# Another order of all instructions for a dilated convolution with a gate, on one core

## Chip, cores and metric

The kernel runs on one core of a Trainium2 chip. The time is the device time of one execution in microseconds (us). Five engines work on their own instruction queues, each in order: TensorE (PE in the profile; its weight loads are PEld), VectorE (DVE), ScalarE (ACT), GpSimd (POOL) and SyncE (SP), which here only issues transfers.

## What is computed

```
B, T, D, K = 2, 16000, 256, 3            # x: (B, T, D), w: (K, D, 2D), w_o: (D, D), bf16
h[t] = x[t] @ w[0] + x[t-2] @ w[1] + x[t-4] @ w[2]      # x is zero before its start
f, g = h[..., :D], h[..., D:]
z = tanh(f) * sigmoid(g)
return z @ w_o
```

A causal convolution over time with three taps and dilation 2, for each of the two batches, a gate, and one more product.

## The kernel before

**Groups.** The 32,000 rows are cut into 23 groups (`GROUPS`, `ORDER`). 18 are of kind A (6 x 256 rows), 4 of kind B (4 x 256 rows, the last one 4 x 160) and one, the first, of kind P, done by plain products. A group's input `xt` comes transposed from DRAM by a transfer that SP issues (token `x`), so that channels lie on the partitions.

**Fewer products by sums.** Kinds A and B don't multiply every tap with every row. They form sums and differences of input tiles first and multiply these with combined weights (as in fast convolution by Toom-Cook points), then take the outputs apart again. For a group of kind A the tiles are `u0, u1, u2, e, f` (differences and sums of two views of `xt`), three scaled copies of `u1` (`u3` = u1/3, `uh` = -u1/2, `ud` = 2 u1), and four tiles made on top of others: `rp` = f + u1, `rm` = e + u3, `r0` = u0 + uh, `ri` = u2 + ud. Each tile is 128 x 1024. The scaled copies are DVE's (L329). A sum is one DVE instruction of 128x1024 or four GpSimd pieces of 128x256 (L331), the pieces held until a named DVE instruction is done. The four "on top" tiles are mostly made by a transfer that GpSimd issues and that adds its source onto the tile in SBUF (L326, `u<-uh` and the like in the profile).

**Products.** Every group has four blocks (one per 128 columns of `h`). A block of kind A is five products of two matmuls 128x512 on PE (L360): F (`wa` x u1), M (`wm` x rm), L (`wp` x rp), Z (`w[2]` x r0) into a PSUM bank `b`, and I (`w[0]` x ri) into a bank `a`. Between them the banks are read: ACT copies `b` to `ss` (token `c`, L391); the sum `a` = 3 ss + b (token `A`, L394, DVE), the second product `hh` and the sum `yy` (token `Y`, L394, DVE). `hh` has two forms: `h`, a DVE sum 1.5 ss - b, or `k`, a plain copy of `b` by ACT (L404):

```python
if on_act:
    G["k", oi] = True
    nc.scalar.copy(out=G["hh", oi][:, :n], in_=G["b", oi][:, :n])
    return
stt(G["hh", oi][:, :n], G["ss", oi][:, :n], 1.5, G["b", oi][:, :n], ALU.subtract)
...
if ("k", oi) in G:
    stt(G["y", oi][:, :n], G["hh", oi][:, :n], -2.0, G["a", oi][:, :n])
else:
    stt(G["y", oi][:, :n], G["hh", oi][:, :n], 2.0, b)
```

With `k` the sum `yy` reads bank `a` (and I, which adds to that bank, stands behind it); with `h` it reads bank `b` (and Z stands behind it). ACT then takes tanh or sigmoid of `b`, `yy` and `a` (L442; `th`, `sg`), DVE multiplies the two to `zz` (the gate, token `g`, L461), PE multiplies `zz` with `w_o` (token `P`, four matmuls 128x256, L479), ACT or DVE takes the result out of PSUM (tokens `e` on ACT, L496; `v` on DVE, L488) and SP stores it. PSUM has two banks for `a`, three for `b`, three for `o_ps`.

**What sets the order.** A list written out by an offline planner, `PLAN`, of some 1,730 tokens. The kernel goes through it once and emits each token's instructions; every engine runs its own in that order, and semaphores, derived from who reads and writes which tile, hold an instruction until its inputs and its buffer are free. A token with `q` and a number is one GpSimd piece, with how far back the DVE instruction lies that it is held behind; a token that ends in `d` is an adding transfer. So the list sets the order on each engine and the splits (DVE or GpSimd, `h` or `k`, `e` or `v`), not times.

Of the kernel before, what the change touches and what calls it, by code (L numbers as in the profile page):

```python
# [23 lines left out]
d3.2q11 L A d3.2q12 Z I g b Z p.2 a I b m.2 F d3.2q1 P A c F ri.0d rp.0 a I e2 e.0 L e3 Z uh.0 c wa.14q1 P A b rm.0d  # L24
P d0.2 e4 Z a g I s2 e5 F s0 u1.1 x b L u2.1 d3.2q1 P c A F a L u0.0 wa.10q34 c Z A I b wa.8q3 L u1.2 a Z uh.1 F b
ud.1 wa.3q1 I A c F r0.0d g a x L c u0.1 Z e6 P u2.2 b M u3.1 I ud.2 k0 F g wa.5q1 a L A c P wa.13q47 e7 A Z
wa.15q25 e8 M wa.11q2 Y b I wa.9q4 s3 k1 f.1 Z ri.1d a F e.1 L c g I rm.1d b M A rp.1d F k2 f.2 r0.1d P c Y P y M
e.2 a L h3 e9 u1.3q1 Z A y I u1.3q3 L b Y P u1.3q27 a Y F e10 u1.3q55 I A c ri.2d Z e11 u3.2 M e.3 b rm.2d Z uh.2 y
rp.2d F g b P c u0.2 F k4 M f.3 r0.2d a I h5 c L u0.3q41 y P A rp.3d M a u0.3q46 L Y e12 P k6 Y Z y A I b L u3.3 e13
I ud.3 rm.3d g a F Z c u1.4q17 A P y M u1.4q51 Y b P u1.4q77 v14 k7 Z a F e.4 s7 b L x g I c f.4q70 F y A M c  # L30
u0.3q49 v15 P k8 M f.4q9 Y a L h9 f.4q61 e16 Z x e17 A f.4q44 P b L u1.4q53 Y I e18 uh.3 F a u2.4q73 Y Z c P u0.3q32
A b I u2.3 r0.3d y Z u3.4 F y g rm.4d M b I c h10 F e19 u0.4 M a L h11 e.5q85 c P y A ri.3d P e20 L Y e.5q55 M a s9
Y I x k12 u2.4q96 A Z a P f.5 b L u1.5 e21 Z e22 F A I b u3.5 P c Y u2.5q56 F y g rp.4d M c Z u2.4q21 y h13 P b M
uh.4 u2.5q32 a L h14 F e23 u2.5q18 Y I c s10 e.5q60 L A s8 a M u1.6q97 Y e24 P e.5q67 y h15 Z e25 I u2.4q35 A P b
rp.5d e.6 L y r0.4d F g a Z c I uh.5 f.6q1 b A P a M ud.4 u2.5q107 e26 F Y P k16 ri.4d u0.5 s11 Z c g L r0.5d b P
f.6q61 e27 A I y M v29 e28 P u2.6q119 Y a F u2.6q111 h17 P c rm.5d Z ud.5 y L u0.6 ri.5d b M A f.6q110 e30 P Y e31 F
I h18 c u1.6q41 I e32 g M u2.6q35 a Z s13 a h19 x L b P u1.6q62 A L y f.6q34 Y F y I u1.6q22 A c Z u2.6q28 e33 Y P y
rp.6d e.7 P s12 b M g a Z F y h20 u0.7q138 I b u3.6 L c u2.7q95 F A e34 u2.7q119 P e35 Y M rm.6d c P s14 ud.6 a u1.7
Z ri.6d k21 M uh.6 I b g r0.6d P e36 u2.7q79 L h22 a P e37 A F u2.7q30 y L Y u0.7q38 c P A e38 Z u0.7q22 y Y I s15 M
b x ud.7 P u3.7 a e.8q13 h23 Z e39 F g b L c I A e.8q1 e41 F y Y M f.7q56 I c u1.8 rm.7d Z k24 x uh.7 M v40 b  # L40
u0.8q38 L a h25 P f.7q64 y P A u0.7q84 e42 F Y P a L c f.8 f.7q1 Z e44 A I b e.8q8 Y M a F f.7q33 v43 k26 Z g c
rp.7d I b L ri.7d ud.8 M a uh.8 r0.7d F y A P k27 u1.9 P u0.8q1 c Y L y M A u0.8q141 e45 Z y P Y e.8q10 I b e.9
rp.8d Z k28 f.9 F a I u3.8 b L g rm.8d c F e46 u0.8q94 A M c P h29 a u0.9q113 M Y e47 L u0.9q24 y P h30 s18 u2.9q173
Z e48 s17 A I s16 r0.8d b Y x L e49 F g a Z u1.10q148 c P Y b M u3.9 u0.9q156 e50 A I y F u0.9q35 h31 Z a uh.9 L c
e.10 I y f.10q121 A P a M u2.9q126 Y b P u1.10q64 h32 y Z s19 g y r0.9d P F e51 rp.9d ud.9 L b u2.8 P f.10q1 c F A x
e52 I Y c f.10q61 M e53 ri.8 Z u1.10q41 a M h33 b I u2.9q193 h34 y L rm.9 F a P Y c u1.11q130 L e55 A u1.10q159 P y
M A u2.9q40 e56 s20 Z Y I ri.9d b g Z k35 I ud.10 b F v54 L a u0.10 F s21 u1.11q1 c P x A c P uh.10 a f.11q177 M Y
e57 M f.10q205 h36 y Z k37 I u3.10 g L b u1.11q1 L e58 A F a P f.11q30 Y y I u1.11q125 A c Z a rm.10d P Y e59 M
r0.10d e.11 b P s22 rp.10d u2.10 Z k38 I e60 g F b L u0.11 c u1.12q203 P e61 A M e62 F u2.11 u1.12q10 y P h39 c P
f.11q159 Y P e63 M e64 uh.11 ri.10 Z a r0.11d L h40 b u1.12q70 P e65 A I y F Y s24 f.11q59 a L x v66 u1.12q202 Z c A  # L50
I b M uh.12 a F u3.11 k41 Y I rm.11d c g L rp.11d y Z u2.12q144 y A P s23 P a Y M b ud.11 Z k42 f.12 ri.11d F e67 g
L c u1.13q10 I b A M e68 P ud.12 u2.12q170 k43 Y F s25 a P x e.13q141 v69 L c u1.13q192 v70 Z y M A u1.13q56 b I h44
u1.13q143 y F y Y u2.12q33 P c L f.13 Z a u3.12 M e.12 b P k45 g I rm.12d e71 P u2.12q47 Y a L s26 y F A u2.13q9 P
e72 A Z c ri.12d uh.13 I b ud.13 M Y e73 e.13q1 F a h46 Z rp.12d c I u0.12 b L g r0.12d M a F u2.13q107 A k47 P c L
u3.13 u0.13q227 y Y I e74 M e.13q243 A e75 Z s27 e.14q133 h48 P b Y P e.13q204 y F f.14 rm.13d a Z g c L rp.13d I b
u0.13q19 Y P e77 F A a M u2.14q139 v76 c Z e78 u0.13q220 h49 M s28 b I x u1.14 e.14q65 y L h50 F a e.14q155 A P y L
c u0.13q34 Y I e79 A u2.13q15 M y Z Y e.14q244 a P g rp.14d b Z I k51 r0.13d uh.14 F e80 u3.14 L e.15 b P c A
f.15q119 F e81 ud.14 P u2.13q157 y Y M c u0.14 P ri.13d e82 Z u1.15 rm.14d k52 M g I a L b u2.15q51 h53 P a F A
f.15q193 e83 L c u2.15q120 Y s30 P y s29 P A f.15q228 x y M Y u2.14q124 Z e84 h54 I u2.14q230 y Z g b f.15q1 L b F Y
a I u2.14q32 c F A e85 P ri.14d u3.15 y M u1.16 r0.14d Z c h55 P b uh.15 M u0.15q1 a v87 I e86 F g u0.15q123 k56 L  # L60
s31 c P x Y P y u0.15q60 A M e88 u2.15q270 L a h57 Z f.16q173 y A I b u2.15q92 L Y e89 P f.16q46 a Y F s32 u0.15q60
# [586 lines left out]
```

## Time and profile before

| | |
|---|---|
| median of 3 runs | 259.36 us (259.35 to 259.39) |
| profiled execution | 259.23 us, of which the span from first to last instruction is 257.4 us |
| granted TensorE clock | 0.998 |
| busy in the span | PE 250.3, DVE 242.4, ACT 242.4, POOL 179.5 us |
| adding transfers (256 KB each, issued by GpSimd) | 67 |
| transposing loads / stores (issued by SP) | 22 / 46 |

How to read it: a matmul's record lasts longer than the time until the next one starts, since matmuls overlap, so a busy PE can still have lost time; a stall shows as starts that lie further apart than usual. A wait is put down to what ended last. DVE's and ACT's records overlap a little too. Transfers have a time from issue to landing.

### The profile page before, as it was taken

Reading aid. Unit: us, or ns where it says so; the run is one execution under the profiler, and the core shown is the slowest. Engines: PE = TensorE matmul, PEld = TensorE weight load, DVE = VectorE, ACT = ScalarE, POOL = GpSimd, SP = SyncE. Lnnn points to the kernel's source line nnn. Section 1 sums busy time; section 2 is a strip of 40 time slices with the busy share of each in tenths; the row PEclk is TensorE's granted clock in tenths of the full one; section 3 lists DMA queues with packets and bytes.
Section 4 is the critical chain, followed back from the end, with each engine's and each line's share of the span. In section 5 each row is a group of like instructions: output and inputs, shape, how many; then the busy total and the mean of one; then the engine's idle time right before and its main releaser. Section 6 shows DMA issues by size and latency. Waiting matters only on the chain.

```text
span 257.4 us, 4566 instructions
## 1 busy us (share of the span) xinstructions
PE 250.3 (97%) x1428; PEld 137.8 (54%) x1428; DVE 242.4 (94%) x405; ACT 242.4 (94%) x488; POOL 179.5 (70%) x256
## 2 busy tenths in 40 slices
PE   8999999999999999999999999999999999999992
PEld 4644545555555555554554555554555554555681
DVE  2898999999999999999999999999999999999991
ACT  5968999999999999999999999999999999999993
POOL 1133658869689988797886968699899899970000
PEclk9999999999999999999999999999999999999999
DMA  6999899989999999999999989998999986673425
GB/s 186 207 201 219 180 209 242 173 147 194 190 272 273 183 200 278 195 209 214 243 196 288 245 168 201 299 245 179 190 244 243 223 180 135 192 120 131 168 108 190
DMA packets 84752, 52.51 MB, mean 204 GB/s; under 512 B 69080, under 2 KB 70360, under 8 KB 84728
## 3 DMA queue, kind: packets, MB, share of 16 engines
q1 hardware_dynamic: 74168, 33.71, 54.3%
q0 software_dynamic: 9648, 17.57, 40.1%
q10 hardware_dynamic: 912, 0.95, 1.2%
q8 instruction: 11, 0.18, 0.3%
q14 instruction: 13, 0.11, 0.1%
HBM read 1.25 MB, written 16.38 MB: 68 GB/s over the span
## 4 chain that ended last, share of the span: by engine, by line
PE 68%; DVE 9%; POOL 6%; ACT 6%; DMA 5%; issue 3%; ACTq 0%; DVEq 0%; POOLq 0%
PE b L360 40%; PE o_ps L479 14%; PE a L360 10%; DMA e<-u 3%; DMA u<-uh 3%; POOL f L331 2%; ACT sg L442 2%; DVE a L394 2%; DVE yy L394 2%; POOL u L331 2%; PE b L380 1%; PE a L380 1%; ACT osb L496 1%; ACT th L442 1%; ACT ss L391 1%
## 5 line engine op out<-in xcount | busy, mean ns | idle before, releaser
L331 POOL TENSOR_TENSOR u<-xt 128x256 bf16<-128x256 bf16 x92 | 70.1, 775 | 7.8 <-PE a L360 2.4
L479 PE MATMUL o_ps<-wo_sb,zz 128*128 128x256 bf16 x496 | 70.9, 273 | 0.0
L496 ACT CAST osb<-o_ps 128x512 bf16<-128x512 f32 x102 | 62.1, 626 | 0.8 <-PE o_ps L479 0.7
L479 PEld LDWEIGHTS <-zz 128*128 128x128 bf16 x496 | 48.3, 98 | 26.6 <-DVE zz L461 0.4
L394 DVE SCALAR_TENSOR_TENSOR a<-ss,b 128x512 f32<-128x512 f32 (+1 forms) x88 | 59.2, 678 | 2.7 <-PE b L360 1.9
L391 ACT COPY ss<-b 128x512 f32<-128x512 f32 (+1 forms) x88 | 53.3, 608 | 1.1 <-PE b L360 0.6
L360 PEld LDWEIGHTS <-w_sb 128*128 128x128 bf16 x352 | 34.0, 97 | 37.1 <-issue 2.2
L360 PE MATMUL b<-u,w_sb 128*128 128x512 bf16 x144 | 42.8, 379 | 0.4 <-DMA u<-uh 0.2
L360 PE MATMUL b<-f,wp_sb 128*128 128x512 bf16 x144 | 42.6, 379 | 0.3 <-DVE hh L394 0.3
L360 PE MATMUL b<-e,wm_sb 128*128 128x512 bf16 x144 | 42.6, 379 | 0.3 <-DMA e<-u 0.2
L360 PE MATMUL b<-u,wa_sb 128*128 128x512 bf16 x144 | 42.8, 379 | 0.0
L360 PE MATMUL a<-u,w_sb 128*128 128x512 bf16 x144 | 42.2, 379 | 0.0
L461 DVE TENSOR_TENSOR zz<-th,sg 128x1536 bf16<-128x1536 bf16 (+2 forms) x46 | 40.6, 884 | 0.0
L442 ACT ACTIVATE th<-b 128x512 bf16<-128x512 f32 (+1 forms) x44 | 26.9, 612 | 3.8 <-PE b L360 2.2
L394 DVE SCALAR_TENSOR_TENSOR hh<-ss,b 128x512 f32<-128x512 f32 x43 | 29.2, 680 | 1.0 <-PE b L360 0.9
L394 DVE SCALAR_TENSOR_TENSOR yy<-hh,b 128x512 f32<-128x512 f32 x43 | 29.1, 678 | 0.0
L442 ACT ACTIVATE sg<-b 128x512 bf16<-128x512 f32 (+1 forms) x44 | 27.2, 619 | 0.8 <-PE b L360 0.5
L442 ACT ACTIVATE sg<-a 128x512 bf16<-128x512 f32 (+1 forms) x44 | 27.8, 632 | 0.2 <-PE a L360 0.2
L442 ACT ACTIVATE th<-a 128x512 bf16<-128x512 f32 (+1 forms) x44 | 27.0, 615 | 0.4 <-PE a L360 0.3
L331 POOL TENSOR_TENSOR f<-xt 128x256 bf16<-128x256 bf16 x32 | 24.8, 782 | 3.0 <-PE b L360 2.0
L360 PEld LDWEIGHTS <-wp_sb 128*128 128x128 bf16 x176 | 17.2, 98 | 17.9 <-issue 2.9
L360 PEld LDWEIGHTS <-wm_sb 128*128 128x128 bf16 x176 | 17.0, 97 | 14.8 <-issue 1.0
(68 smaller groups left out, 363.0 us busy)
## 6 DMA issues: line engine op xcount, KB each, us to landing
out_dram<-osb SPq DMA_DIRECT2D x36, 384.0 KB, 3.5
e<-u POOLq DMA_DIRECT2D x17, 256.0 KB, 4.1
u<-uh POOLq DMA_DIRECT2D x17, 256.0 KB, 5.4
f<-u POOLq DMA_DIRECT2D x17, 256.0 KB, 5.0
u<-ud POOLq DMA_DIRECT2D x16, 256.0 KB, 4.2
out_dram<-osb SPq DMA_DIRECT2D x8, 256.0 KB, 3.9
w_sb<-in_w_dram ACTq DMA_DIRECT2D x3, 256.0 KB, 4.1
xt<-in_x_dram SPq DMA_TRANSPOSE x22, 8.2
```

The source lines that it names most:

```text
L331: ins = eng.tensor_tensor(out=o, in0=a, in1=b, op=op)
L360: nc.tensor.matmul(G[bank, oi][:, :2 * R], lhsT=wmat[:, ct, osl], rhs=G[mv][:, :, ct, :R], start=which == "first" and ct == 0, stop=ct == ...
L380: nc.tensor.matmul(G[bank, oi][:, :4 * r].rearrange("p (j r) -> p j r", j=4), lhsT=w_taps[tap][:, ct, osl], rhs=xt[:, j0:j0 + 4, ct, c0 + ...
L391: nc.scalar.copy(out=G["ss", oi][:, :n], in_=G["b", oi][:, :n])
L394: return note(nc.vector.scalar_tensor_tensor(out=out, in0=in0, scalar=scalar, in1=in1, op0=ALU.mult, op1=op))
L442: nc.scalar.activation(out=G[name, dt][:, j:j + 2, :R], in_=G[bank, oi][:, :2 * R].rearrange("p (q r) -> p q r", q=2), func=(ACT.Tanh, ACT ...
L461: note(nc.vector.tensor_tensor(out=G["z"][:, dt, :, :n], in0=G["th", dt][:, :, :n], in1=G["sg", dt][:, :, :n], op=ALU.mult))
L479: nc.tensor.matmul(o_ps[:, q, :], lhsT=z, rhs=wo_sb[:, dt, :], start=dt == 0 and (q == 0 or len(dts) == NT), stop=dt == NT - 1, skip_group ...
L496: copy(out=G["osb", at][:, 2 * jp:2 * jp + 2, :], in_=o_ps[:])
```

## The change

Only `PLAN` is replaced; all code, groups and buffers are as before (the new text has one line less, so line numbers in it are lower by one). Its first lines:

```diff
 PLAN = """
-p.0 m.0 d0.0 d3.0 F F c G D w D L c wa.1q1 F A wa.2q4 L c wa.7q5 Z A wa.4q4 I b d3.1 L a F d0.1 I m.1 c Z a A D
-wa.0q1 L x d p.1 wa.12q1 Z b A I b F G Z g c P b u1.0 F a I f.0 e0 L ud.0 a F u2.0 x P c u3.0 P wa.6q1 c A L e1
...
+m.0 d3.0 p.0 F F d0.0 c D c G D L w L A D wa.2q4 F A wa.0q3 d Z c G I b d3.1 L a Z m.1 F d0.1 b wa.4q1 I c A P
+wa.6q11 a F p.1 L c x g I wa.7q1 L A a Z u1.0 P b f.0 I wa.1q1 e0 Z A a P wa.3q11 F b u3.0 rp.0d Z ud.0 c g F L x
...
```

PE has the same matmuls in another order. Counted over the two lists, the splits change so:

| | before | now |
|---|---|---|
| second products as DVE sums (`h`) / ACT copies (`k`) | 43 / 29 | 38 / 34 |
| results taken out by ACT (`e`) / DVE (`v`) | 104 / 22 | 101 / 25 |
| full sums 128x1024 on DVE | 70 | 71 |
| sums for the 160-row group on DVE (128x640) / in GpSimd pieces (128x160) | 0 / 16 | 1 / 12 |
| GpSimd pieces 128x256 | 148 | 148 |
| adding transfers | 67 | 66 |

**At the start, DVE.** The sums for the first group of kind B (`p`, `m`, `d`), the gate of the first group P (`zo`, `zz`, from `th_182,sg_184` and `th_206,sg_208`) and the first sums `a`. Before:

```order
L457 TENSOR_TENSOR zo<-th_182,sg_184 128x128
L461 TENSOR_TENSOR zz<-th_182,sg_184 128x4x128
L394 SCALAR_TENSOR_TENSOR a<-ss,b 128x512 x2
L331 TENSOR_TENSOR d_287<-xt 128x1024
L331 TENSOR_TENSOR d_295<-xt 128x1024
L331 TENSOR_TENSOR m<-xt 128x1024
L394 SCALAR_TENSOR_TENSOR a<-ss,b 128x512
L331 TENSOR_TENSOR p<-xt 128x1024
L394 SCALAR_TENSOR_TENSOR a<-ss,b 128x512
L457 TENSOR_TENSOR zo<-th_206,sg_208 128x128
L461 TENSOR_TENSOR zz<-th_206,sg_208 128x4x128
```

Now:

```order
L456 TENSOR_TENSOR zo<-th_182,sg_184 128x128
L460 TENSOR_TENSOR zz<-th_182,sg_184 128x4x128
L393 SCALAR_TENSOR_TENSOR a<-ss,b 128x512 x2
L456 TENSOR_TENSOR zo<-th_206,sg_208 128x128
L460 TENSOR_TENSOR zz<-th_206,sg_208 128x4x128
L330 TENSOR_TENSOR d_290<-xt 128x1024
L330 TENSOR_TENSOR m<-xt 128x1024
L330 TENSOR_TENSOR d_302<-xt 128x1024
L393 SCALAR_TENSOR_TENSOR a<-ss,b 128x512
L330 TENSOR_TENSOR p<-xt 128x1024
```

The second gate of group P moved from behind four sums of input tiles and two sums `a` to the place right behind the first two sums `a`.

**At the start, ACT.** The first copies and activations of the first group of kind B (`th_285,sg_305` before, `th_288,sg_304` now). Before:

```order
L391 COPY ss<-b 128x512
L442 ACTIVATE sg_305<-a 128x512
L436 ACTIVATE sg_208<-a 128x4x80
L442 ACTIVATE sg_305<-b 128x512
L442 ACTIVATE th_327<-b 128x512
L391 COPY ss<-b 128x512
L442 ACTIVATE sg_345<-b 128x512
L442 ACTIVATE th_327<-a 128x512
```

Now:

```order
L435 ACTIVATE sg_208<-a 128x4x80
L390 COPY ss<-b 128x512
L441 ACTIVATE th_288<-b 128x512
L441 ACTIVATE th_288<-a 128x512
L441 ACTIVATE sg_304<-b 128x512
L390 COPY ss<-b 128x512
L441 ACTIVATE sg_304<-a 128x512
L390 COPY ss<-b 128x512
L441 ACTIVATE th_340<-a 128x512
L441 ACTIVATE th_340<-b 128x512
```

Before, the first activation into the next `th` tile (`th_327`) follows the last of the tile ahead (`sg_305`) directly; now a copy `ss` stands between them, and the last activation of group P (`sg_208`) stands ahead of the first block's activations instead of among them.

**In the middle, GpSimd.** The stretch of pieces and adding transfers for groups of kind A some 80 us into the run. Before:

```order
L326 DMA u_963<-ud 128x1024
L331 TENSOR_TENSOR e<-xt 128x256
L331 TENSOR_TENSOR u_943<-xt 128x256
L331 TENSOR_TENSOR u_1080<-xt 128x256
L326 DMA f<-u_832 128x1024
L331 TENSOR_TENSOR u_943<-xt 128x256
L331 TENSOR_TENSOR u_1080<-xt 128x256 x2
L331 TENSOR_TENSOR e<-xt 128x256
L331 TENSOR_TENSOR u_1137<-xt 128x256
L331 TENSOR_TENSOR e<-xt 128x256
L331 TENSOR_TENSOR u_943<-xt 128x256
L326 DMA f<-u_1053 128x1024
```

Now:

```order
L325 DMA e<-u_972 128x1024
L325 DMA u_978<-uh 128x1024
L325 DMA u_1027<-ud 128x1024
L330 TENSOR_TENSOR u_988<-xt 128x256
L330 TENSOR_TENSOR f<-xt 128x256
L330 TENSOR_TENSOR u_1146<-xt 128x256
L330 TENSOR_TENSOR e<-xt 128x256 x2
L325 DMA f<-u_821 128x1024
```

The transfer `f<-u_821`, whose tile PE reads from its 457th matmul on, is GpSimd's 77th instruction now (pieces, transfers and the fills at the start counted); ahead of it stand three transfers together and five pieces, where before transfers and pieces alternated. Before, the transfer that PE needs nearest to that place (`f<-u_832`, from its 455th matmul on) is GpSimd's 66th.

**At the end, GpSimd.** The last adding transfers and the pieces for the last group (`p`, `m`, `d` of 128x160). Before:

```order
L331 TENSOR_TENSOR u_3188<-xt 128x256 x2
L331 TENSOR_TENSOR e<-xt 128x256
L331 TENSOR_TENSOR f<-xt 128x256
L331 TENSOR_TENSOR p<-xt 128x160
L331 TENSOR_TENSOR e<-xt 128x256 x3
L326 DMA f<-u_2995 128x1024
L326 DMA e<-u_3267 128x1024
L326 DMA u_3271<-ud 128x1024
L331 TENSOR_TENSOR u_3188<-xt 128x256
L331 TENSOR_TENSOR m<-xt 128x160
```

Now:

```order
L330 TENSOR_TENSOR u_3090<-xt 128x256
L330 TENSOR_TENSOR f<-xt 128x256
L330 TENSOR_TENSOR e<-xt 128x256 x2
L330 TENSOR_TENSOR f<-xt 128x256
L325 DMA e<-u_3008 128x1024
L325 DMA f<-u_2990 128x1024
L325 DMA u_3130<-uh 128x1024
L330 TENSOR_TENSOR p<-xt 128x160
L330 TENSOR_TENSOR d_3293<-xt 128x160
L330 TENSOR_TENSOR u_3090<-xt 128x256
L330 TENSOR_TENSOR d_3308<-xt 128x160 x3
```

The transfer onto `e` for the last group of kind A is now GpSimd's 234th instruction, not its 252nd: the pieces of the last group follow it, where before most preceded it, and it is PE's 1,275th matmul that reads the tile first (the 1,283rd before).

More of the change, by code (lines that the diff above doesn't have):

```diff
@@ L27 @@
[L27 to L61, printed above, removed]
```

62 lines of the change are left out of this document (48 added, 14 removed).

## Prediction

> **What bounds the kernel now.** I read the page's busy line first, then the busy times by stage.
>
> ```profile
> PE 250.3 (97%) x1428; PEld 137.8 (54%) x1428; DVE 242.4 (94%) x405; ACT 242.4 (94%) x488; POOL 179.5 (70%) x256
> 0.00:20.00 20.00, 19.06 (x119) 10.70 (x120) 14.14 (x25) 14.32 (x30) 3.91 (x14) 1.00 0.91 195
> 20.00:60.00 40.00, 39.62 (x214) 20.49 (x212) 39.10 (x68) 38.43 (x78) 27.55 (x39) 1.00 1.02 196
> 60.00:120.00 60.00, 59.71 (x337) 32.70 (x336) 59.23 (x100) 59.91 (x121) 50.64 (x71) 1.00 1.11 218
> 120.00:180.00 60.00, 59.95 (x335) 32.45 (x334) 59.86 (x102) 58.86 (x119) 49.75 (x67) 1.00 1.07 232
> 180.00:235.00 55.00, 54.39 (x305) 29.32 (x305) 53.95 (x87) 53.68 (x108) 47.62 (x68) 1.00 0.86 180
> ```
>
> Columns by stage are PE, PEld, DVE, ACT and POOL. From 20 us on three engines are busy 96 to 100% of the time, at the full granted clock; POOL has room until 180 us and little after (47.62 of 55). The matmul's own pace says how much of PE's time is lost:
>
> ```profile
> 8.62 2.50 PE a L380 x18
> 99.19 0.59 PE L360 MATMUL b<-u,wa_sb 128*128 128x512 bf16 x2
> 99.62 0.59 PE L360 MATMUL b<-f,wp_sb 128*128 128x512 bf16 x2
> 100.05 0.60 PE L479 MATMUL o_ps<-wo_sb,zz 128*128 128x256 bf16 x4
> 100.49 0.59 PE L360 MATMUL b<-u,w_sb 128*128 128x512 bf16 x2
> 4.88 2.62 PE b L380 x18
> 251.14 1.47 PE L479 MATMUL o_ps<-wo_sb,zz 128*128 128x256 bf16 x12
> ```
>
> The pairs start 0.43 us apart, so a 512-wide matmul takes 0.215 us; four 256-wide ones take 0.44, so 0.11 each; a 320-wide one 2.50/18 = 0.139. The program has 816 of the first (72 blocks of kind A with 10, 12 full ones of kind B with 8), 500 of the second and 80 of the third: 175.4 + 55.0 + 11.1 = 241.5 us. From 4.88, where the products start, to the last start at some 252.4 are 247.5 us. So PE loses about 6.0 us to waiting (0.3 of it are eight small transposes), spread thinly, and that is all that an order can win; PE's work itself stays. The largest single losses, as the timeline shows them:
>
> ```profile
> 18.81 0.60 ACT L442 ACTIVATE th<-b 128x512 bf16<-128x512 f32 x1 [0.97 <-DVE zz L461]
> 22.38 1.08 PE L360 MATMUL b<-p,wp_sb 128*128 128x512 bf16 x4 [0.39 <-ACT ss L391]
> 200.85 0.61 PE L360 MATMUL b<-u,w_sb 128*128 128x512 bf16 x2 [0.23 <-DMA u<-uh]
> 217.31 0.60 PE L479 MATMUL o_ps<-wo_sb,zz 128*128 128x256 bf16 x4
> 218.02 0.60 PE L360 MATMUL b<-e,wm_sb 128*128 128x512 bf16 x2
> 230.19 0.60 PE L479 MATMUL o_ps<-wo_sb,zz 128*128 128x256 bf16 x4
> 230.97 0.59 PE L360 MATMUL b<-e,wm_sb 128*128 128x512 bf16 x2 [0.17 <-DMA e<-u]
> ```
>
> A bracket is idle time after the last matmul's modelled end, which lies 0.16 us (0.59 - 0.43) behind the pace, so the loss is the bracket plus 0.16: 0.55 at 22.38 and 0.39 at 200.85. At 218.02 and 230.97 the starts lie 0.71 and 0.78 behind four matmuls that take 0.44: 0.27 and 0.34. The other 4.4 us are many waits of a tenth of a microsecond, in which PE, DVE and ACT hold each other.
>
> **Part 1, the start.** PE's wait at 22.38 goes back to ACT, which had stood 0.97 us at 18.81 until the gate of the first group was done on DVE; behind it ACT ran without a pause to the copy `ss` that PE waits for. The list puts that gate ahead of four sums of DVE's, so ACT finds its tile free. Gain at most 0.55, all of PE's wait. Loss at most 0.47: the gate's two instructions now stand ahead of the sums `d` that PE's next products read, and they take
>
> ```profile
> L461 DVE TENSOR_TENSOR zz<-th,sg 128x512 bf16<-128x512 bf16 x4 | 1.7, 418 | 0.0
> L457 DVE TENSOR_TENSOR zo<-th,sg 128x128 bf16<-128x128 bf16 x4 | 0.9, 220 | 0.1
> ```
>
> 0.42 + 0.22 by record, 0.47 by starts (0.34 + 0.13). I take -0.45, near the gain, since PE has products of the same block to run meanwhile.
>
> **Part 2, the transfers at the end.** The chain of waits runs through GpSimd there, from 183 us on:
>
> ```profile
> 187.44 0.71 POOL u L331
> 193.69 0.58 POOL u L326
> 194.27 6.53 DMA u<-uh
> 210.25 1.16 POOL p L331
> 214.66 3.31 DMA e<-u
> 226.82 4.01 DMA e<-u
> ```
>
> GpSimd's pieces take the time, then the transfer that they held back, and then PE is late. How far GpSimd had come at a given matmul is read from counts:
>
> ```profile
> 0.00:79.50 79.50, 78.17 (x439) 41.73 (x440) 72.64 (x124) 72.21 (x146) 47.19 (x75) 1.00 1.02 206
> 79.50:82.50 3.00, 3.00 (x19) 1.73 (x18) 3.00 (x7) 3.00 (x7) 2.68 (x5) 1.00 1.05 192
> 82.50:174.10 91.60, 91.26 (x514) 49.90 (x513) 90.80 (x154) 90.41 (x182) 76.41 (x103) 1.00 1.10 228
> 174.10:226.80 52.70, 52.26 (x292) 28.14 (x291) 51.69 (x82) 51.67 (x105) 49.64 (x70) 1.00 0.89 191
> 226.80:229.30 2.50, 2.50 (x17) 1.47 (x15) 2.50 (x6) 2.50 (x6) 1.56 (x4) 1.00 0.82 138
> ```
>
> (An instruction over a border counts on both sides.) By 226.8 us GpSimd had begun some 250 instructions, and the transfer onto `e`, its 252nd, was the last that PE could wait for. Now that transfer is the 234th, read at the 1,275th matmul, which ran at 229.3: 16 instructions of some 0.7 us (49.64/70), or 11 us, of room. Counted so, transfer by transfer, all from 190 us on have at least five instructions of room now, where before half had three or fewer. The three losses sum to 0.39 + 0.27 + 0.34 = 1.0 and should go. Late next are DVE and ACT: of 55 us they had 1.05 and 1.32 idle, hardly more than the gain. Gain 0 to 1.0; I take -0.7. GpSimd's own four pieces and one transfer less (2 + 0.9 us by its pieces here) lie off the path.
>
> **Part 3, the transfers in the middle.** The opposite holds about 60 and 80 us. The transfer `f<-u_821` is the 77th, and PE reads its tile at the 457th matmul, 82.5 us into the run. At 3.31 from issue to landing, the shortest in the chain above, it must be issued by 79.2, but by 79.5 GpSimd had begun only 75. Two instructions more are 1.4 us, the bound of the loss; the other end is 0, if GpSimd waits less than the 2.18 us that it lost just ahead:
>
> ```profile
> 71.90 0.68 POOL L331 TENSOR_TENSOR u<-xt 128x256 bf16<-128x256 bf16 x1 [2.18 <-PE a L360]
> ```
>
> Some of that wait will stay, since pieces are still held until PE and DVE are done with tiles. I take +0.3, nearer to 0. About 61, 91 and 93 us the same count leaves none to spare.
>
> **Part 4, second products and results.** Pace by starts on a full engine:
>
> ```profile
> 41.88 0.59 ACT L404 COPY hh<-b 128x512 f32<-128x512 f32 x1 [0.18 <-PE b L360]
> 42.38 0.59 ACT L391 COPY ss<-b 128x512 f32<-128x512 f32 x1
> 102.33 0.68 DVE L394 SCALAR_TENSOR_TENSOR hh<-ss,b 128x512 f32<-128x512 f32 x1
> 102.93 0.95 DVE L461 TENSOR_TENSOR zz<-th,sg 128x1536 bf16<-128x1536 bf16 x1
> ```
>
> A second product is 0.50 on ACT and 0.60 on DVE; a result taken out I price the same. ACT: 5 more copies, 3 fewer results, +1.0. DVE: 5 fewer sums, 3 more results, -1.2, one sum 128x1024 and one 128x640 more, some +1.0 at most, so about -0.2. GpSimd's and PE's parts are done above. On the path lies between 0 and the whole 1.0 of ACT, which had 0.09 idle from 60 to 120 us and 1.14 from 120 to 180; below 0 it can't go, since DVE gains almost nothing. I take +0.2, since a full engine slips only where PE stands behind it.
>
> The Trainium skill, "Perfetto Trace Analysis", section "Identifying the Most-Contended Engine", speaks against the change: it says to improve the engine with the highest occupancy first, and for VectorE and ScalarE the occupancy is to be trusted. The trace has both at 94%, and the list loads one of them further; by that rule the whole of ACT's +1.0 would count and nothing of the rest would be won, 260.4. Rival (a) below is this kernel's own form of it.
>
> **Sum.** -0.45 - 0.7 + 0.3 + 0.2 = -0.65. The profiled run took 259.23 us (0.13 under the median of 259.36): 258.6 there, 258.7 as a median.
>
> **Rivals.** (a) ScalarE becomes the bound. Counted in the new order, the 969th matmul, which ran at 174.1, needs ACT's 337th instruction done; by the counts above ACT had begun 333 then (146 + 7 + 182, less two counted twice), the last two under way. So ACT must be some six instructions, 3 us, further at the same place. It had 1.57 + 0.09 + 1.14 = 2.8 us idle from 20 to 180 us and 5.7 ahead of 20. If it can't, PE waits for what is missing: with half of it, +1.5 and without the +0.2, 259.36 - 0.85 + 1.5 = 260.0, slower. It decides if ACT still idles over 0.5 us between 60 and 180. Against it: ACT starts its stretch earlier by part 1. Chance 0.18. (b) Transfers in the middle are late: the four places at 61, 82, 91 and 93 us cost the bound of 1.4 once and 0.4 at each other, +2.6 instead of +0.3: 261.0. It decides if two of the four cost more than 0.5. For it: the counts; against it: GpSimd had idle time ahead of 80 us. Chance 0.10. (c) Nothing is won: what PE doesn't wait for a transfer it waits for DVE or ACT, both full, 259.4. Chance 0.24. (d) The three engines hold each other less: of the 4.4 us of small waits a third goes, -1.5 more: 257.2. For it: all small waits are the order's; against it: no row tells that the new order has fewer. Chance 0.13. My sum keeps 0.35.
>
> **How the numbers follow.** Changes under 0.2%, 0.5 us, are about what cannot be told from none here. Under 258.84 lie most of my forecast (0.28 of 0.35), (d) and a little of (c): 0.44. Over 259.88 lie (b), most of (a) and a little of (c): 0.28. The rest, 0.28, is no change. From 257.0 to 260.7 leaves half of (b) and the outer ends of (d) and (a) out. The forecast's own range is 257.8 (parts 1 and 2 at their gain ends, 3 and 4 at nothing) to 259.4 (part 3 at 1.0).
>
> **What would show it.** Part 1: no wait of ACT for `zz` near 19 us, no PE wait for `ss` near 22. Part 2: no PE wait for a transfer after 190 us, and the chain leaving GpSimd there. Part 3: a wait of PE for `f<-u` near 82 us. Part 4: ACT's busy time up by some 0.6 to 1.0 us. It would be wrong if PE's lost time between 40 and 180 us moved by more than 1 us in either direction, which no row of mine decides.

## The result, and the profile after

The changed kernel takes 261.07 us (median of 15 runs, 259.89 to 263.17) against 259.41 for the kernel before on the same chips (259.20 to 260.01). The ratio is 1.0059, with a 95% interval of 1.0045 to 1.0073: slower by 1.5 us, where 0.7 less was forecast. Its runs also scatter four times as far. The profiled execution is one of the longer ones: 261.78 us, span 259.9. Medians, ranges and ratios of the experiments below leave out executions over 1.5% longer than the fastest one of the same kernel.

The page's busy line, and the stages of the prediction's table from 20 us on:

```profile
PE 251.2 (97%) x1428; PEld 138.5 (53%) x1428; DVE 243.7 (94%) x405; ACT 243.2 (94%) x490; POOL 181.2 (70%) x251
20.00:60.00 40.00, 38.56 (x210) 20.08 (x208) 38.59 (x68) 37.41 (x76) 29.99 (x40) 1.00 1.07 195
60.00:120.00 60.00, 59.59 (x329) 31.74 (x327) 59.60 (x101) 59.44 (x121) 46.57 (x62) 1.00 1.06 210
120.00:180.00 60.00, 59.67 (x339) 32.84 (x338) 59.33 (x99) 59.61 (x122) 50.39 (x67) 1.00 1.09 224
180.00:235.00 55.00, 54.38 (x301) 29.00 (x300) 53.63 (x87) 53.45 (x107) 46.53 (x65) 1.00 0.95 205
```

The clock is full, and but for the second stage the busy times hardly differ from those before: a table like this does not show where 2 us are lost. The matmuls that came latest do, in PE's timeline:

```profile
36.73 0.61 PE L359 MATMUL b<-e,wm_sb 128*128 128x512 bf16 x2 [1.32 <-DMA e<-u]
117.41 0.59 PE L359 MATMUL b<-u,wa_sb 128*128 128x512 bf16 x2 [0.37 <-ACT th L441]
144.87 0.59 PE L359 MATMUL b<-u,w_sb 128*128 128x512 bf16 x2 [0.32 <-DMA u<-uh]
182.79 0.59 PE L359 MATMUL a<-u,w_sb 128*128 128x512 bf16 x2 [0.26 <-DVE a L393]
225.72 0.60 PE L359 MATMUL b<-u,w_sb 128*128 128x512 bf16 x2 [0.33 <-DVE a L393]
```

The largest is a transfer. The chain of waits shows its whole length, and GpSimd's timeline when it was issued:

```profile
26.72 0.84 POOL wa_sb L233
27.55 9.13 DMA e<-u
36.68 0.05 issue
36.73 0.61 PE b L359 x2
...
27.55 0.88 POOL L325 DMA_DIRECT2D e<-u  x1
```

The same transfer, at the same time of the kernel before, landed in 3.3 us. This is the view of the DMA queues from 27 to 29.5 us, in the kernel before and then now (KB, and us from the start of the issue to the landing):

```profile
e<-u POOLq DMA_DIRECT2D x1, 256.0 KB, 3.3
e<-u POOLq DMA_DIRECT2D x1, 256.0 KB, 9.1
```

What is around it differs. SP issued the sixth and seventh transposing load in a row now (SP's timeline gives six loads from 7.63 to 32.46 us, then the stores); before, the seventh stood behind two stores and was issued at 30.3. From 28.5 to 32 us the queues of the changed kernel read:

```profile
DMA packets 1206, 0.31 MB, mean 89 GB/s; under 512 B 1205, under 2 KB 1205, under 8 KB 1205
q1 hardware_dynamic: 1205, 0.30, 97.3%
q14 instruction: 1, 0.01, 2.5%
xt<-in_x_dram SPq DMA_TRANSPOSE x1, 10.4
```

q1 carries loads and stores, q0 GpSimd's transfers. GpSimd was done with the issue at 28.43, and for the next 3.5 us q0 has no packet at all. The Trainium skill, "DMA: Bandwidth & Descriptors", section "Queues, rings and completion order", says that each DMA engine alternates, packet by packet, between the queues that have work for it; this trace doesn't look like that, though it can't show whether the transfer's descriptors were late or the engines kept to the load.

To see where the 2.5 us of span went, every matmul's start was set against the pace of the matmul before it (0.216, 0.136 and 0.109 us by width), and the excess summed by stretch. Two further profiles of the unchanged new list and four experiments stand beside it:

```
us of PE lost      0-10 10-30 30-40 40-140 140-150 150-180 180-200 200-220 220-end  from 10 on
before             2.01  0.93  0.20   1.89    0.10    0.76    0.19    1.12    0.38     5.57
changed            2.71  0.07  1.49   2.46    0.68    0.49    0.77    0.06    1.04     7.06
 second look       2.49  0.06  0.00   2.58    1.04    0.49    0.76    0.06    1.03     6.02
 third look        2.07  0.05  0.00   2.52    1.22    0.50    1.96    0.06    1.20     7.51
thin stores (e5)   2.97  0.06  0.00   2.47    0.25    0.48    0.27    0.10    0.74     4.37
no 13 copies (e8)  2.03  0.05  0.00   2.45    0.26    1.34    1.76    0.06    0.89     6.81
one load (e17)     2.26  0.05  2.09   2.48    0.49    0.49    0.79    0.06    0.98     7.43
load+add (e18)     2.89  0.07  0.52   2.48    0.25    0.64    0.85    0.06    0.98     5.85
```

For the first profile 1.49 from 10 us on, 0.70 ahead of 10 us (the first group's products, the same in both lists; the looks differ there by 0.6) and 0.29 from the last matmul to the end make the 2.48 by which the spans differ. Read down the columns: 10 to 30 and 200 to 220 us gain 0.9 and 1.0 or more in every run of the new list. 40 to 140 loses 0.6 in every run, and 220 to the end 0.4 to 0.8. The losses at 30 to 40, 140 to 150 and 180 to 200 us jump, also between executions of one program.

What stays the same from look to look is mostly no late transfer. Between 40 and 140 us the waits over 0.1 us that end with ScalarE sum to 1.6 us in each of the three looks, against 0.5 before; those that end with VectorE to 0.3 to 0.5, against 0.9. The wait at 117.41 (0.53 by the pace) is in all three, and in e5 and e8. At 182.79 and 225.72 (0.42 and 0.49 by the pace) PE waits for a sum that stands behind a gate of VectorE's. Such a gate usually takes 0.95 us. These two took 1.49 and 1.42, with GpSimd's pieces beside them:

```profile
180.64 1.49 DVE L460 TENSOR_TENSOR zz<-th,sg 128x1536 bf16<-128x1536 bf16 x1
223.04 1.42 DVE L460 TENSOR_TENSOR zz<-th,sg 128x1536 bf16<-128x1536 bf16 x1
```

In e5 the first of the two took 0.98 us, and PE's wait at 182 us is absent.

### The profile page after: what moved, and what is told of

It is laid out like the page before. It is cut to its first block, busy times and chain, and to the rows that moved or that the text cites. A ratio compares the mean times of both kernels' runs of the same rounds, so it can differ in the third digit from the quotient of the medians.

```text
span 259.9 us, 4558 instructions
## 1 busy us (share of the span) xinstructions
PE 251.2 (97%) x1428; PEld 138.5 (53%) x1428; DVE 243.7 (94%) x405; ACT 243.2 (94%) x490; POOL 181.2 (70%) x251
## 4 chain that ended last, share of the span: by engine, by line
PE 52%; DVE 13%; ACT 12%; POOL 10%; DMA 7%; issue 4%; ACTq 0%; POOLq 0%; DVEq 0%
PE b L359 30%; PE o_ps L478 12%; PE a L359 7%; POOL u L330 5%; DVE a L393 4%; DMA e<-u 4%; ACT sg L441 3%; ACT th L441 3%; ACT osb L495 2%; DVE yy L393 2%; ACT ss L390 2%; DMA u<-uh 2%; POOL f L330 2%; DVE zz L460 2%; POOL u L325 1%
## 5 line engine op out<-in xcount | busy, mean ns | idle before, releaser
L330 POOL TENSOR_TENSOR u<-xt 128x256 bf16<-128x256 bf16 x80 | 61.8, 790 | 8.7 <-issue 3.7
L495 ACT CAST osb<-o_ps 128x512 bf16<-128x512 f32 x99 | 63.6, 664 | 0.7 <-PE o_ps L478 0.7
L390 ACT COPY ss<-b 128x512 f32<-128x512 f32 (+1 forms) x88 | 55.6, 637 | 2.2 <-PE b L359 1.4
L330 POOL TENSOR_TENSOR f<-xt 128x256 bf16<-128x256 bf16 x40 | 31.3, 791 | 6.9 <-PE b L359 5.0
L441 ACT ACTIVATE th<-b 128x512 bf16<-128x512 f32 (+1 forms) x44 | 28.5, 648 | 1.2 <-PE b L359 0.4
L441 ACT ACTIVATE sg<-b 128x512 bf16<-128x512 f32 (+1 forms) x44 | 28.7, 652 | 0.7 <-PE b L359 0.5
L441 ACT ACTIVATE sg<-a 128x512 bf16<-128x512 f32 (+1 forms) x44 | 29.0, 659 | 0.2 <-PE a L359 0.2
L441 ACT ACTIVATE th<-a 128x512 bf16<-128x512 f32 (+1 forms) x44 | 28.5, 647 | 0.3 <-PE a L359 0.3
L325 POOL DMA_DIRECT2D u<-uh x17 | 17.9, 1055 | 12.3 <-issue 5.0
L393 DVE SCALAR_TENSOR_TENSOR hh<-ss,b 128x512 f32<-128x512 f32 x38 | 25.7, 681 | 0.6 <-PE b L359 0.5
```

The costliest lines, as they stand in the source:

```text
L325: return settle(nc.gpsimd.dma_start(out=G[name][:, :, :, :R], in_=b, accum_op=op), False)
L330: ins = eng.tensor_tensor(out=o, in0=a, in1=b, op=op)
L390: nc.scalar.copy(out=G["ss", oi][:, :n], in_=G["b", oi][:, :n])
L393: return note(nc.vector.scalar_tensor_tensor(out=out, in0=in0, scalar=scalar, in1=in1, op0=ALU.mult, op1=op))
L441: nc.scalar.activation(out=G[name, dt][:, j:j + 2, :R], in_=G[bank, oi][:, :2 * R].rearrange("p (q r) -> p q r", q=2), func=(ACT.Tanh, ACT ...
L495: copy(out=G["osb", at][:, 2 * jp:2 * jp + 2, :], in_=o_ps[:])
```

## The experiments

T (sharpened to T' and T'') is the theory that late landings of transfers make the loss; its rivals have names of their own. A token `x` is a load, `s0` a store.

**Loads, first.** The seventh load behind the first store; and, in the kernel before, the seventh load ahead of its stores.

```diff
e1, changed kernel:  - u0.0 c P x c d0.2 ... F e5 s0 L      + u0.0 c P c d0.2 ... F e5 s0 x L
e2, kernel before:   - I s2 e5 F s0 u1.1 x b L              + I x s2 e5 F s0 u1.1 b L
```

> The changed kernel with one transposing load (the seventh, which SP issued at 27.2 us right behind the sixth) moved behind the first store, so that SP issues it at some 33 us; nothing else is moved. Theory T (the adding transfer of rm.0, e<-u, issued at 27.55, lands 8.25 us after its issue because its packets are served behind those of two transposing loads in a row): it lands within 4 us of its issue, the wait of 1.48 us of PE at 36.7 us goes, the median falls by 1.0 to 1.5 us to 259.6 to 260.1, and the runs scatter by under 1 us as those of the kernel before do, not by 3.3. Rival R (the loads are innocent, the transfer is slow for a reason of its own, or the loss is spread over many small waits): landing still over 6 us, or the wait goes and the time moves by less than 0.4.

> The kernel before with its seventh transposing load moved ahead of two stores, right behind the sixth, as in the changed kernel (issued at some 25 instead of 30.3 us). Theory T: the adding transfer e<-u, issued at 28, lands 5 to 8 us after its issue instead of 2.47; there PE has 4.6 us of margin, so the time rises by 0 to 1.5 us (259.4 to 260.9) and the scatter grows if the landing goes over the margin. Rival R: it lands within 4 us as before, 259.4.

e1: 260.62 us (259.61 to 262.56), ratio 1.0060 (1.0037 to 1.0084), no gain. The edit did less than planned: SP reached the moved load at 27.36 us, not at 33, so that it stood 0.3 us behind the transfer instead of 0.3 ahead of it. At its place the theory held: the transfer landed after 5.2 us and PE didn't wait. But in this profile VectorE stood for a load at 184.83, which had taken 10.93 us, then needed 1.16 us instead of 0.42 for a scaled copy with GpSimd beside it, and PE lost 1.58 us at 189.33:

```profile
27.36 5.62 SPq L167 DMA_TRANSPOSE xt<-in_x_dram  x1
173.78 10.93 DMA xt<-in_x_dram
184.83 0.70 DVE L330 TENSOR_TENSOR u<-xt 128x1024 bf16<-128x1024 bf16 x1 [0.76 <-DMA xt<-in_x_dram]
186.12 1.16 DVE L328 TENSOR_SCALAR uh<-u 128x1024 bf16<-128x1024 bf16 x1
189.33 0.59 PE L359 MATMUL a<-u,w_sb 128*128 128x512 bf16 x2 [1.42 <-DVE yy L393]
```

e2: 260.25 us, ratio 1.0045 (1.0029 to 1.0061). One load moved in the old list costs 1.0 us against the 259.29 of the kernel before on that chip. The transfer `e<-u` took 6.7 us instead of 3.3 and was still in time; the next one, `u<-uh`, with little margin, was not:

```profile
e<-u POOLq DMA_DIRECT2D x1, 256.0 KB, 6.7
40.62 0.60 PE L360 MATMUL b<-u,w_sb 128*128 128x512 bf16 x2 [0.94 <-DMA u<-uh]
```

**Single waits taken away.** The late transfer as a sum of VectorE's; and a scaled copy earlier, for the transfers at the end.

```diff
e3:  - A a rm.0d F u0.0            + A a rm.0 F u0.0
e4:  - F rp.16d g a I ... L uh.16 b F      + F rp.16d uh.16 g a I ... L b F
```

> The changed kernel with the one adding transfer of rm.0 taken by a sum of VectorE's (128x1024, 0.60 us by starts); the loads stay. Theory T: the wait of 1.48 us at 36.7 us goes, DVE has 0.6 more on a full stretch, so 0.6 to 1.4 less than the changed kernel, 259.7 to 260.5, and the next transfer, r0.0 (landing 6.45 us after its issue, margin 1.59 us), is now the one that could be late. Rival R (spread loss): -0.3 to +0.6 against the changed kernel, 260.8 to 261.7.

> The changed kernel with one scaled copy of VectorE's (uh of the seventeenth group of kind A) some eight of its instructions earlier, at 216.5 instead of 219.3 us, so that GpSimd, which stood 3.94 us ahead of the transfer u<-uh at 220.98, can issue it by 217.5. Theory T2 (my room of 16 instructions at the end was eaten by this wait of GpSimd's): PE's waits for transfers at 225.7, 228.2 and 232.3 us go (0.49 + 0.20 + 0.17, less the usual 0.1 or so of each), 0.3 to 0.8 less than the changed kernel, 260.3 to 260.8. Rival (VectorE and ScalarE are late there too): less than 0.2 either way, 260.9 to 261.3.

e3: 262.51 us (260.91 to 264.69), a miss: the wait at 36.7 went, and in the profile PE stood 1.86 us at 228.98 for `u<-ud` and 0.99 at 144.21. e4: 260.82 us (260.65 to 261.32), ratio 1.0059 (1.0044 to 1.0074), no gain. `u<-uh` was issued at 216.72 instead of 220.98 as planned, and the wait at 225.7 went. But GpSimd's next two pieces (from 217.28 and 218.37 us) now ran beside a sum of input tiles and a scaled copy of VectorE's instead of beside its reads of PSUM and the gate at 223.04, and these took twice as long:

```profile
217.49 1.37 DVE L330 TENSOR_TENSOR u<-xt 128x1024 bf16<-128x1024 bf16 x1
218.78 0.89 DVE L328 TENSOR_SCALAR ud<-u 128x1024 bf16<-128x1024 bf16 x1
221.51 0.59 PE L359 MATMUL a<-u,w_sb 128*128 128x512 bf16 x2 [0.70 <-DVE yy L393]
```

0.68 and 0.42 are usual. The Trainium skill, "SBUF — State Buffer", section "Who interferes with whom", describes this: VectorE and GpSimd share a pair of ports under an exclusive lock, which a VectorE instruction needs in its two-port modes, or with two inputs in SBUF while GpSimd reads SBUF too, and the later of the two waits in full. The rows agree (1.37 for 0.68, 0.89 for 0.42).

**The transfers' load, and ScalarE.** Stores that write one row of six (or of four), in both kernels; six loads ahead of stores; thirteen ScalarE copies left out.

```diff
e5, e6:  - dma_start(out=to, in_=osb[:])     + dma_start(out=to[:, J-1:J, :], in_=osb[:, J-1:J, :])
e7:      - s27 e75 I x M        + x s27 e75 I M        (this load and five others)
e8:      - nc.scalar.copy(out=hh, in_=b)     + hh = ss           (13 of 34)
```

> The changed kernel with every store of a full tile writing one of its six (or four) rows per partition, 64 instead of 256 or 384 KB; the rest of the output isn't written. Number and order of all instructions stay. Theory T' (the new order reads tiles close behind their transfers' landings, and landings vary from 2.4 to 8 us with what else the transfer engines carry, so now one, now another transfer is late): landings get shorter, the waits of PE for transfers mostly go, 0.8 to 1.6 us less than the changed kernel (259.5 to 260.3), runs scatter by under 1.5 us. Rival C (the loss lies between PE, ScalarE and VectorE, not in the transfers): less than 0.4 gained, 260.7 or more.

> The same cut of the stores in the kernel before. Theory T': its reads stand further behind the landings, so it gains less than the changed kernel does, 0 to 0.6 us (258.7 to 259.3), and the distance between the two orders shrinks from 1.7 to under 0.8 us. Rival C: both gain alike, and the distance stays 1.3 us or more.

> The changed kernel with six of its transposing loads each put ahead of the one or two stores that stood directly ahead of them in SP's queue; their buffers had been free 12 to 18 us before (at 156.5 us for the load issued at 174.9, whose tile VectorE reads 10.2 us later). Theory T': in the traces of two other versions of this order that load landed 10.9 us after its issue, and VectorE, and behind it PE, lost 1.4 to 1.6 us; this cannot happen any more, so 0.3 to 0.9 us less in the median than the changed kernel, 260.2 to 260.8. Rival: the stores, now behind the loads, hold up ScalarE's buffers or the adding transfers, no gain, 261 to 261.7.

> The changed kernel without the thirteen ScalarE copies that are second products there and sums of VectorE's in the kernel before (21 of 72 second products changed side, 13 of them to ScalarE); the sum that read the copy reads the first copy ss in its place, so the output differs. ScalarE has 13 x 0.5 = 6.5 us less to do, nothing else changes. Rival (a) of the prediction (ScalarE is the bound): 1.5 us or more less than the changed kernel, under 259.6. Theory T': only PE's waits for ScalarE go (0.27, 0.18, 0.53, 0.18 and 0.16 us between 50 and 180 us in the trace, less 0.1 each that any wait has), 0.3 to 1.0 less, 260.1 to 260.8, and the scatter stays.

e5: 258.23 us, ratio to the kernel before 0.9952 (0.9935 to 0.9970), 2.8 less than the changed kernel. Of this, 1.1 us are the end alone: the last, shorter store lands sooner, and from the last matmul's start to the end 4.30 us pass instead of 5.39. Landings are shorter (page, issues; of the changed kernel first, then e5), and the waits at 36.7, 144 and 182 us are gone:

```profile
e<-u POOLq DMA_DIRECT2D x18, 256.0 KB, 5.1
u<-ud POOLq DMA_DIRECT2D x17, 256.0 KB, 5.1
xt<-in_x_dram SPq DMA_TRANSPOSE x22, 7.8
...
e<-u POOLq DMA_DIRECT2D x18, 256.0 KB, 4.1
u<-ud POOLq DMA_DIRECT2D x17, 256.0 KB, 4.3
xt<-in_x_dram SPq DMA_TRANSPOSE x22, 6.7
```

e6: 260.17 us, ratio 1.0025 (0.9998 to 1.0052), a miss: the old list doesn't gain, though its end is shorter by 1.1 us too, and it scatters from 258.14 to 261.95. The record doesn't show why. With light stores the new list is ahead by 1.9 us.

e7: 281.99 us, ratio 1.086, a miss. These six loads ahead of their stores are the worst order of all. One of them was issued at 192.72; six adding transfers issued behind it landed 17 to 18.5 us after their issue, and PE stood 11.45 us. Meanwhile little was moved: this is the queue view of e7 from 203 to 206 us, and of the changed kernel from 25 to 28, where a load ran nearly alone:

```profile
DMA packets 353, 0.23 MB, mean 75 GB/s; under 512 B 277, under 2 KB 277, under 8 KB 353
q0 software_dynamic: 82, 0.16, 84.5%
q1 hardware_dynamic: 271, 0.07, 65.2%
210.88 1.01 PE L359 MATMUL b<-u,w_sb 128*128 128x512 bf16 x2 [11.45 <-DMA u<-uh]
...
DMA packets 2669, 0.73 MB, mean 244 GB/s; under 512 B 2640, under 2 KB 2640, under 8 KB 2669
```

The packets' times sum to more than the stretch (84.5 and 65.2%), and yet the two kinds of transfer together move a third of what a load moves.

e8: 261.14 us, against 261.07 with the copies, a miss for T'. ScalarE is busy 4.6 us less, and nothing comes of it:

```profile
PE 249.7 (96%) x1428; PEld 138.0 (53%) x1428; DVE 244.1 (94%) x405; ACT 238.6 (92%) x477; POOL 182.3 (70%) x251
```

**Plain loads, and parts of the change.**

```diff
e9, e10:  - nc.sync.dma_start_transpose(out=xt, in_=x)       + nc.sync.dma_start(out=xt, in_=x)     (same bytes)
e11, kernel before:  - c Z a A D wa.0q1 L x d p.1 ... F G Z g     + F A D wa.2q4 L c wa.7q5 d Z A G wa.4q5 ...
e12:  x behind s0 (as e1);  f.13 rp.13d;  f.11q27 r0.9d;  uh.16 u0.17
```

> The changed kernel with the 22 loads taken by plain instead of transposing transfers: the same bytes into the same tiles, laid out wrongly, so that the output differs; all other instructions and their order stay, the stores are full size again. Theory T'' (transfers that add and loads that transpose slow each other where they overlap: over nine profiles an adding transfer issued alone landed after 2.5 us in the median, one issued into a transposing load after 4.3, at most 10.2; the new order has more reads close behind such landings): landings stay under 5 us, PE's waits for transfers at 36.7, 144 to 146 and 188 us go, 1.2 to 2.5 us less than the changed kernel (258.6 to 259.9), runs within 1 us of each other. Rival S (the number of bytes is what counts, as the thinner stores suggest): landings stay as they are, less than 0.5 gained.

> The same plain loads in the kernel before. Theory T'': it gains less than the changed kernel, 0 to 0.8 us (258.6 to 259.4), since its reads stand further behind the landings; the new order is then no slower than the old, and faster by 0.3 or more if its shorter small waits (1.8 to 2.8 us in the profiles against 3.0 before) come through. Rival S: both unchanged, the old order still ahead by 1.3 us or more.

> The kernel before with part 1 of the change alone: the gate of the first group P, with the last products and the activation that it needs, moved ahead of the sums d, d, m and p of the next group, as the new list has it. The prediction's part 1: ACT's wait of 0.97 us at 18.8 and PE's of 0.55 at 22.4 us go, -0.45 (0 to -0.55), so 258.8 to 259.1 against some 259.4. Rival: everything behind is shifted by half a microsecond against the loads and the adding transfers, and another transfer is late in its place: no gain, 259.3 to 260.

> The changed kernel with four moves that take adding transfers out of the transposing loads or give them room: the seventh load behind the first store (as in the first experiment); the transfer f<-u of the fourteenth group of kind A directly behind its sum (issued at some 171 instead of 176 us, ahead of the load issued at 174.9); the transfer u<-uh of the tenth group three GpSimd pieces earlier (138.3 instead of 140.06); the scaled copy uh of the seventeenth group two VectorE instructions earlier (218.4 instead of 219.3). Theory T'': the waits at 36.7, 144.9, 188 and 225 us go, 0.6 to 1.3 us less than the changed kernel, 259.8 to 260.5, less scatter. Rival: others of the dozen transfers with under 1 us of margin are late in their place, less than 0.4 gained, 260.7 to 261.2.

e9: 259.91 us, ratio 1.0013 (0.9998 to 1.0028), 1.2 less than the changed kernel; e10: 260.31, 1.0033 (1.0022 to 1.0044), 0.7 more than the old list, a miss. So the new list is ahead again, by some 0.4 us, though the intervals overlap a little. Theory T'' was too narrow. The waits at 36.7, 144 and 188 us went as it said (the first because the plain loads were over by then), but PE stood 1.07 us at 70.64 for a transfer that overlapped two plain loads and landed 7.6 us after its issue, and 1.13 us at 227.40 for one that overlapped no load, only stores and other adding transfers (5.7 us). So overlap makes a transfer late without any transposing, in this one profile.

e11: 259.81 us, 1.0007 (0.9996 to 1.0019). The wait at 22.4 went, and PE stood 0.68 us at 18.63 for a sum `a` of VectorE's instead:

```profile
18.63 0.59 PE L360 MATMUL b<-d,w_sb 128*128 128x512 bf16 x2 [0.68 <-DVE a L394]
```

e12: 261.45 us (261.18 to 263.32), ratio 1.0088 (1.0060 to 1.0115), a miss. The seventh load stood later in the list, but SP reached it at 26.39 us, sooner than in the changed kernel and 0.8 us ahead of the transfer. This took 9.9 us, PE stood 2.08 us for it at 37.12, and the third move made another piece late (0.54 at 142.64).

**Adding transfers cut, two more looks, one load.**

```diff
e13, e14:  - dma_start(out=G[name][:, :, :, :R], ...)     + dma_start(out=G[name][:, :, 0:1, :R // 2], ...)
e17:  - u1.11q89 s20 L x I        + u1.11q89 x s20 L I
e18:  as e17, and  - f.13 L ... Z c rp.13d g     + f.13 rp.13d L ... Z c g
```

> The changed kernel with every adding transfer cut to a quarter of its bytes (128x2x128 instead of 128x1024 elements; three quarters of the sums stay unmade, so the output differs). GpSimd issues the same number of transfers at the same places in all lists, loads and stores are whole. Theory T (late landings of adding transfers are the loss): landings fall to 2 to 3 us, no wait of PE for one, 1.5 to 3 us less than the changed kernel, 258.0 to 259.6, runs within 1.2 us. Rival C (the order on the engines is the slower one): less than 0.7 gained, 260.4 or more.

> The same cut in the kernel before. Theory T: it gains 0.5 to 1.2 us (its three losses at 200.9, 218.0 and 231.0 us are 1.0 together), 258.2 to 259.0, and the new order is level with it or ahead by up to 1 us. Rival C: the new order stays behind by 1.3 us or more.

> The changed kernel as it is, another profile. Theory T (chance decides which transfer is late): the wait of 1.48 us at 36.7 us is gone or of another size, and one or two other places (70, 144, 188 or 225 to 229 us) have lost more than in the first profile. Rival (a fixed fault of the order): the same waits at the same places within 0.2 us.

> As the look before: theory T says other waits again, the rival the same ones.

> The changed kernel with one transposing load (issued at 136.6 us behind a store that waited 5 us for its tile; its buffer was free at 123.6) moved ahead of that store, so that it is issued at some 131.5 us and is over when the transfer u<-uh of the tenth group is issued at 140. Theory T (overlap): that transfer lands within 3 us of its issue instead of 3.8 to 4.4, PE's loss between 140 and 150 us falls from 0.7 to 1.2 to about 0.25, the median by 0.4 to 0.9 (260.2 to 260.7). Rival: the load then meets the adding transfers issued at 132.7, or the store behind it holds up ScalarE, and the loss only changes its place: 260.8 to 261.6.

> As the run before, and the transfer f<-u of the fourteenth group directly behind its sum (171 instead of 176 us), so that the load issued at 174.9 runs alone and VectorE finds its tile at 185. Theory T: the loss between 180 and 200 us falls to 0.3 to 0.8 in every run, 0.3 to 0.6 less in the median than the run before (259.7 to 260.3). Rival: as before, 260.8 or more.

e13: 268.92 us, e14: 272.31 us. Both misses: a transfer of 128x2x128 elements takes GpSimd 1.53 us to issue, one of 128x1024 takes 0.94, so GpSimd's pieces moved beside VectorE's sums, and VectorE was busy 253.0 instead of 243.7 us. Groups of GpSimd, changed kernel and e13:

```profile
L325 POOL DMA_DIRECT2D e<-u x18 | 16.9, 939 | 2.6 <-issue 1.3 <-DVE e L330 0.9 <-POOL e L330 0.3
...
L325 POOL DMA_DIRECT2D e<-u x18 | 27.5, 1529 | 1.8 <-DVE e L330 1.3 <-issue 0.3
```

The landings did shorten, from 4.0 to 2.2 us in the mean (counted from the end of the issue), but the runs tell nothing on their price. The new list is ahead of the old one here too, by 3.4 us.

e15 and e16 (260.51 and 261.57 us, one execution each): the wait at 36.7 is gone in both, the one at 143 to 145 is there in all three looks, 0.5 to 1.0 us, and one look in two has lost 1.3 at 188.6. Both theories were half right: some waits are the order's, some come and go. The one at 188.6 is not a load's alone: in e16 VectorE stood only 0.24 us for its load, and then a sum took 1.64 us instead of 0.68 beside a GpSimd piece. e16's VectorE and PE:

```profile
143.30 0.59 PE L359 MATMUL b<-u,w_sb 128*128 128x512 bf16 x2 [0.85 <-DMA u<-uh]
185.51 1.64 DVE L330 TENSOR_TENSOR u<-xt 128x1024 bf16<-128x1024 bf16 x1
188.60 0.59 PE L359 MATMUL a<-u,w_sb 128*128 128x512 bf16 x2 [1.12 <-DVE yy L393]
```

e17: 261.39 us (259.72 to 263.13), ratio 1.0072 (1.0043 to 1.0101), e18: 260.61 us, ratio 1.0053 (1.0025 to 1.0082), neither to be told from the changed kernel's 1.0059; both missed what T gave. In the table the moved load does what it should (140 to 150 us: 0.49 and 0.25), but in both profiles the transfer at 27 us was late (9.7 and 8.2 us), and e17's lost 2.09 us there alone. No version here beat the kernel before with all its work done.

The transfer at 27 us looks like chance. In the eleven profiles of new lists that issue it whole and with transposing loads, it took 5.2, 6.2, 6.2, 6.5, 6.7, 6.7, 8.2, 9.1, 9.3, 9.7 and 9.9 us. PE needs it 7.7 us after its issue: five of eleven are late. But these five are just those in which SP began to issue the seventh load 0.3 to 1.3 us ahead of the transfer. Where the load began less than 0.1 us ahead of the transfer, or behind it, or at least 1.7 us ahead, the transfer took 5.2 to 6.7 us. In the three looks at one program the load began 0.33, 1.68 and 0.07 us ahead, and the transfer took 9.1, 6.2 and 6.7. This is a pattern of eleven profiles; no experiment moved the load by such steps.

## Why the prediction was wrong

**Part 1** came out by more than its number, but not by its mechanism. ACT's wait for `zz` at 18.8 and PE's at 22.4 us are gone, and 10 to 30 us lost 0.07 instead of 0.93. The gate alone (e11) brought nothing: what it won at 22.4 came back as 0.84 us at 18.63, the loss that was bounded at 0.47 and taken as near nothing. The gain is that of the whole new start. Which part of it made it no run shows, so the number was luck.

**Part 2** is half a miss. 200 to 220 us gained 1.06, more than the 0.66 of the two waits forecast there, but from 220 us on 0.66 was lost: most of it at 225.72, behind the slowed gate (0.49), and some at 228 us, where a transfer is late again (0.19). The step that failed is the count of "16 instructions, 11 us, of room": it took GpSimd to work through. In the changed kernel it stood 3.94 us ahead of the transfer issued at 220.98, and the 234th instruction began at 227.8, 1.0 us later than the old 252nd. Net -0.4 instead of -0.7. The end behind the last matmul, for which there was no term, is 0.29 longer.

**Part 3** is the term that broke the sum: +0.3 was taken, bound 1.4. The four places named (61, 82, 91, 93 us) cost no wait for a transfer; `f<-u` near 82 us landed 0.82 us ahead of its use. Other places lost 1.3 to 2.7 together in the three looks: 30 to 40 us (-0.2 to 1.3), 140 to 150 (0.6 to 1.1) and 180 to 200 (0.6 to 1.8). In the first two a transfer came late. Of the third, 0.4 is the slowed gate at 180.64, and what jumps is a late load together with a slowed instruction of VectorE's. So the step that failed here is the landing time: the working took one, 3.31 us, "the shortest in the chain". In the changed kernel's profile the 66 transfers took 3.3 to 9.1 us from their issue, 5.0 in the mean, and in the kernel before 3.3 to 7.7, 4.8 in the mean. And the change moved loads and stores on SP, which my text did not price although SP's queue is one of those the list orders; e2 puts the price of one moved load at 1.0 us. That instructions of VectorE slow down beside GpSimd's pieces had no term either.

**Part 4** had the sizes: ACT is busy 0.8 us more (forecast 0.6 to 1.0). On the path the copies count 0, not 0.2 (e8). So rival (a), ScalarE as the bound by its load, falls, and with it the rule of the Trainium skill, "Perfetto Trace Analysis", section "Identifying the Most-Contended Engine", as it was weighed there: with ScalarE 4.6 us less busy the time stayed. But ScalarE's place in the order does count: between 40 and 140 us PE waits 1.1 us more for it and 0.4 to 0.6 less for VectorE, which makes about the 0.6 that every run loses there. The prediction's list of the largest losses had left out a wait of this kind, 0.45 us at 119.74 behind VectorE's `hh`.

**The rivals.** (b) gave the right number, 261.0, and in part the right kind of loss, with 0.10 of the chance, but at places where PE waited for no transfer; that its number fits is luck. (d) came partly true: with thin stores the new list loses 1.2 us less than the old one with whole stores, 4.37 against 5.57, although 40 to 140 us costs 0.6 more in every run. In the three pairs in which stores, loads or adding transfers were changed alike in both lists, the new one was ahead (1.9, 0.4 and 3.4 us). In none of them did the old list gain, which is not explained. The condition for being wrong, a move of more than 1 us between 40 and 180 us, came true in two of three looks: PE's loss there rose from 2.75 to 3.63, 4.11 and 4.24.

What stays open: why SP reaches the same load 1.5 us sooner in one execution than in another; why a load issued just ahead of a transfer holds it up most; and why the old list doesn't gain from lighter transfers. That VectorE's slowed instructions cost what the traces put on them was not tested by a run of its own.

## What to carry to other kernels

Where transfers feed the engines at full load, price a new order by the margin between landing and use, with the spread of landings beside every transfer in flight, and follow the loads and stores that the change moves before counting compute instructions. Counting how many instructions an engine has left says nothing on when it gets there, if it waits itself. Look at what runs beside what, too: in e16 a load that VectorE waited 0.24 us for was followed by a sum 0.96 us longer than usual. A list that wins where it was meant to can lose as a whole, and here its scatter was a sign of it.

## What the runs showed of the hardware

- Over fifteen profiles, with everything counted that was in flight when GpSimd was done issuing: an adding transfer with no load and no other adding transfer in flight landed 2.7 us after that moment (median), 3.2 with one other, 4.1 with two, 5.0 with three; with a transposing load and no other adding transfer 3.6, with one in ten over 5.9 and one at 10.2.
- Beside GpSimd's pieces a gate of VectorE's took 1.49 us instead of 0.95 (changed kernel), a sum of 128x1024 1.64 instead of 0.68 (e16) and a scaled copy 1.16 instead of 0.42 (e1).
- A load and several adding transfers together moved 75 GB/s (e7, 203 to 206 us), a load nearly alone 244 (changed kernel, 25 to 28 us).
- An adding transfer of a quarter of the bytes in twice the runs per partition costs GpSimd 1.53 us of issue instead of 0.94.
